# Cluster-masked attention and two feed-forward layers on one NeuronCore: how the centroids, the zero fills and the first heads' low parts are made, and a new table of priorities

## The chip, the core and the metric

The kernel runs on one core of one Trainium2 chip. The metric is the time of one execution in device microseconds, smaller is better; the kernel before takes 782.38 us (median of 3 runs, 782.28 to 784.3). A core has a TensorE for matmuls (PE in the profile, PEld for its weight loads), VectorE (DVE), ScalarE (ACT), GpSimd (POOL) and SyncE (SP), which here only issues DMA transfers. Each engine works through its own queue in order and waits for the others by semaphores.

## The reference

Attention in which a query sees only the keys of its own cluster, and then two feed-forward layers on the 1536 tokens that come out:

```
B, H, S, D, C = 2, 8, 768, 64, 16                  # 16 heads of 768 rows
q_n, k_n, c_n = normalised rows of q, k and the centroids [H, C, D]
q_assign = argmax(q_n @ c_n.T); k_assign = argmax(k_n @ c_n.T)
scores = where(q_assign == k_assign, q @ k.T / sqrt(D), -1e9)
attn = softmax(scores)                             # max subtracted, sum + 1e-9
x = (attn @ v) as [1536, 512]
h = x @ w_in                  # w_in [512, 2048]
x = (h - tanh(h)) @ w_out     # w_out [2048, 512]
out = (sigmoid(x @ w_gate) * (x @ w_val)) @ w_out2 # [512, 1536], [1536, 512]
```

All of it is in float32. The norm of a query row does not change its argmax, so the kernel normalises only the centroids.

## The kernel before

**Precision.** Most matmuls work on two parts: a high part, which is the number cast to a shorter format (fp32r or f16), and a low part, which is the number less its high part. A product is then two or three matmuls. So scores need the high parts of queries and keys (ScalarE, L737 or L748) and the low parts (GpSimd, L741 or L758); probabilities need a high part in f16 (ScalarE's second exponential of a tile) and a low part, which is the first exponential less the high part (L1022 and L1070; GpSimd or VectorE, see below); values need a high part (ScalarE, L913) and a low part (VectorE, L916), both scaled by a power of two `sv` that belongs to the pair of heads.

**Attention.** Work goes by pairs of heads (`pair_prep`, eight times) and then by heads. For a pair, queries and keys are loaded (L710), transposed by TensorE (L721), evacuated by ScalarE (L725), multiplied with the scaled centroids `cb` (L772), and VectorE makes one-hot rows of the largest of 16 scores (L781 to L792). TensorE transposes the one-hot rows (L863), and ScalarE writes them, times a large constant, into the tile `stk` (L867) below the queries and keys: a score matmul over `stk` then gives the masked score in one go. The first pair writes its high and low parts into `stk` straight from ScalarE and GpSimd (L737, L741); the later pairs go by way of `hlq`, `hlk` and DMA copies. The tile `stk_0` and its fellows are zeroed at the start, since the first pair's score matmuls run over rows that nothing writes.

Head 0 is done with queries as rows: for each of six tiles of 128 queries, six matmuls of three terms write the scores into a PSUM bank pair (L1003), VectorE takes the row maximum (L1011), ScalarE does two exponentials with it as bias (L1006), GpSimd or VectorE the low part (L1022), and a DMA transposes the probabilities. The other heads are done with keys as rows: `head_max` computes the maxima beforehand (L936 matmuls, L940 reductions) and adds them to `stk` as a row, so that the score tiles (L1056) need only exponentials (L1059) and low parts (L1070). The products with the values are L1034 for head 0 and L1082 to L1084 for the others. The score tiles and maxima share three bank pairs, `ba`, `bb` and `bc`; `bc` exists only once the first pairs are prepared.

**Centroids.** SP loads the 128x64 tile `cn` (L625); ScalarE squares it and sums its rows, takes the root, and does one exponential on a spare column so that the table of Exp is loaded early (L628 to L630); VectorE adds 1e-6, takes the reciprocal and scales `cn` (L633 to L635); TensorE transposes it (L640), and VectorE places it in `cb` (L645).

**Order.** Every step is a task with an engine, an estimated cost, the tasks that it depends on and the buffers that it takes. `Planner.run` simulates the engines with the estimates and decides which task an engine takes next: among those that could start within a short look-ahead of the earliest one (`AHEAD`, from the `AH_` numbers), the one of least priority number. The priority is read from a table by the task's number,

```
        t.n = len(self.tasks)
        t.prio = ORDER[t.n] / 1000
```

so the priorities given in the code at `add(...)` have no effect. The order that the planner finds is then written out, and each engine runs its own part of it in that order, whatever the real durations are. TensorE is also given 110 tasks of two filler matmuls each on a spare tile (`keep_busy`, L652); they keep it active in the first 50 us.

**What decides who makes a probability's low part.** `FD` and `FO` put every sixth or so of the low parts on VectorE and the rest on GpSimd (`on_v`).

**Feed-forward layers.** L1369 and L1732 are the lines with most of their matmuls; the change touches nothing there but the order.

## Time and profile before

| | |
|---|---|
| median of 3 runs | 782.38 us (782.28 to 784.3) |
| the profiled execution | 784.97 us |
| its span, from the first to the last instruction | 782.8 us |
| mean granted TensorE clock | 0.996 |
| busy in the span: PE / PEld | 770.6 / 728.4 us (98% / 93%) |
| busy in the span: DVE / ACT / POOL | 573.6 / 457.5 / 567.1 us (73% / 58% / 72%) |
| chain that ended last | PE 93%, DVE 5%, ACT 1%, issue 1% |

How to read it: the profile shows one execution, which is a little longer than the median; what lies between its time and its span is start and end. "Busy" counts the time in which at least one instruction of the engine runs. Matmuls are pipelined: the next one starts while the one before is still draining, so TensorE can be shown busy in moments in which it starts nothing; the weight loads are shown apart. The chain of work that ended last is followed back from the last instruction to whatever released it. The granted clock is 1.00 at 2.4 GHz and 0.50 at 1.2 GHz. In the rows an arrow in brackets names the idle time before an instruction and what ended it.

### The profile page before, as it was taken

The numbers are of one execution on the slowest core, as the hardware profiler recorded it, in microseconds if no ns is written. First come the engines' busy times: TensorE is split into PE (matmuls) and PEld (weight loads), VectorE is DVE, ScalarE is ACT, GpSimd is POOL, SyncE is SP. The second block draws the span as 40 slices with busy tenths as digits, with TensorE's granted clock in tenths as the row PEclk, the third lists the DMA queues.
The fourth block names the chain that finished last, engine by engine and source line by source line (L and its number), as shares of the span: only waits on it lengthen the run. The fifth ranks groups of instructions, "written<-read, shape, count | busy, mean of one in ns | idle before, by whom it ended". The sixth has DMA issues, their size and how long they took to land.

```text
span 782.8 us, 15756 instructions
## 1 busy us (share of the span) xinstructions
PE 770.6 (98%) x5905; PEld 728.4 (93%) x5905; DVE 573.6 (73%) x1110; ACT 457.5 (58%) x883; POOL 567.1 (72%) x604
## 2 busy tenths in 40 slices
PE   7999999999999999999999999999999999999998
PEld 6988899898889999999999999999998989899997
DVE  6697878887986978877576878976465786765434
ACT  4588888889887644544554455765462635253250
POOL 6249777778979795787797699699593978665261
PEclk8999999999999999999999999999999999999999
DMA  4597755665642100422131323003220332310004
GB/s 103 133 182 157 165 128 137 145 154 133 152 129 81 59 1 0 135 69 68 54 95 41 108 68 107 14 29 107 68 82 27 98 119 69 93 63 20 1 1 161
DMA packets 75571, 69.57 MB, mean 89 GB/s; under 512 B 39252, under 2 KB 60072, under 8 KB 75496
## 3 DMA queue, kind: packets, MB, share of 16 engines
q1 hardware_dynamic: 75496, 68.58, 32.6%
q8 instruction: 46, 0.75, 0.4%
q14 instruction: 29, 0.24, 0.1%
HBM read 45.12 MB, written 3.15 MB: 62 GB/s over the span
## 4 chain that ended last, share of the span: by engine, by line
PE 93%; DVE 5%; ACT 1%; issue 1%; POOL 0%; DVEq 0%; ACTq 0%; POOLq 0%
PE over_left L1369 17%; PE over_left L1732 15%; PE sm L1732 10%; PE sm L1369 10%; PE over_right L1369 8%; PE over_right L1732 6%; PE bb L1056 3%; PE bc L1056 2%; PE ba L1056 2%; PE sm L1082 2%; PE sm L1083 2%; PE sm L1084 2%; PE sm L772 2%; PE ba L936 1%; DVE finr L940 1%; PE bc L936 1%
## 5 line engine op out<-in xcount | busy, mean ns | idle before, releaser
L1070 POOL TENSOR_TENSOR pt<-pf,pt 128x768 f16<-128x768 f32 x46 | 77.3, 1694 | 19.4 <-ACT pt L1059 9.5
L1070 POOL TENSOR_TENSOR ptt<-pf,ptt 128x768 f16<-128x768 f32 x29 | 49.8, 1723 | 13.4 <-ACT pf L1059 8.2
L1732 PE MATMUL over_left<-xh,stk 128*128 128x384 f32 x186 | 54.7, 335 | 0.0
L1369 PE MATMUL over_left<-stk,w 128*128 128x384 f32 x178 | 46.4, 337 | 0.0
L1082 PE MATMUL sm<-vs,pt 128*128 128x65 f16 x318 | 43.4, 194 | 0.2 <-DVE xl L1121 0.2
L1083 PE MATMUL sm<-vs,pt 128*128 128x64 f16 x318 | 43.2, 195 | 0.0
L1084 PE MATMUL sm<-vs,pt 128*128 128x65 f16 x318 | 42.9, 192 | 0.0
L1748 ACT ACTIVATE pf<-over_left 128x384 f32<-128x384 f32 x40 | 19.6, 489 | 33.0 <-PE over_left L1732 31.7
L940 DVE TENSOR_REDUCE finr<-ba 128x1 fp32r<-128x768 f32 x35 | 33.2, 948 | 5.6 <-PE ba L936 2.7
L1400 ACT ACTIVATE stk<-pf 128x384 fp32r<-128x384 f32 x43 | 22.3, 523 | 25.0 <-POOL pf L1803 6.9
L1402 POOL TENSOR_TENSOR oht<-pf,stk 128x384 fp32r<-128x384 f32 x23 | 23.4, 1018 | 16.5 <-ACT stk L1400 16.5
L1343 POOL TENSOR_TENSOR w<-ry,w 128x256 fp32r<-128x256 f32 x26 | 20.2, 788 | 20.5 <-ACT w L1341 15.9
L1082 PEld LDWEIGHTS <-pt 128*128 128x128 f16 x318 | 29.7, 96 | 5.4 <-issue 5.0
L940 DVE TENSOR_REDUCE finr<-bc 128x1 fp32r<-128x768 f32 x32 | 30.4, 949 | 5.9 <-PE bc L936 5.7
L1732 PEld LDWEIGHTS over_left<-xh,stk 128*128 128x128 f32 x186 | 34.3, 188 | 0.3
L1732 PE MATMUL over_left<-sum,stk 128*128 128x384 f32 x127 | 33.7, 338 | 0.0
L1056 PE MATMUL bb<-stk 112*128 112x384 f32 (+2 forms) x146 | 33.6, 353 | 0.0
L1756 ACT ACTIVATE pf<-pf 128x384 f32<-128x384 f32 x33 | 17.3, 523 | 27.7 <-DVE pf L1752 27.6
L1083 PE MATMUL sm<-vs,ptt 128*128 128x64 f16 x222 | 33.1, 195 | 0.0
L1402 POOL TENSOR_TENSOR stk<-pf,hlk 128x384 fp32r<-128x384 f32 x20 | 21.1, 1056 | 16.6 <-ACT hlk L1400 16.6
L1082 PE MATMUL sm<-vs,ptt 128*128 128x65 f16 x222 | 33.0, 193 | 0.0
L1732 PE MATMUL over_left<-xl,stk 128*128 128x384 f32 x98 | 32.8, 335 | 0.0
(617 smaller groups left out, 3135.2 us busy)
## 6 DMA issues: line engine op xcount, KB each, us to landing
vs<-in_moe_w_out_dram SPq DMA_DIRECT2D x48, 256.0 KB, 2.6
vs<-in_moe_w_in_dram SPq DMA_DIRECT2D x24, 256.0 KB, 2.6
vs<-in_moe_w_val_dram SPq DMA_DIRECT2D x24, 256.0 KB, 2.7
vs<-in_moe_w_gate_dram SPq DMA_DIRECT2D x24, 256.0 KB, 2.9
stk<-hlq SPq DMA_DIRECT2D x28, 192.0 KB, 2.7
stk<-hlk SPq DMA_DIRECT2D x14, 384.0 KB, 4.4
rawq<-in_q_dram SPq DMA_DIRECT2D x16, 192.0 KB, 3.3
rawk<-in_k_dram SPq DMA_DIRECT2D x16, 192.0 KB, 3.7
```

Of the source, the lines that this page charges most:

```text
L940: rd.append(use(mx, add(DVE, c_dve(S), z + t, lambda t=t, mx=mx: nc.vector.tensor_reduce(at(mh)[:, t:t + 1], at(mx)[:, :, 0:HALF], axis=AX ...
L1056: nc.tensor.matmul(o, at(sk)[0:n, l_, ts], at(sk)[0:n, m_, c], start=i == 0, stop=i == len(terms) - 1)
L1070: lambda nce=nc.vector if on_v else nc.gpsimd, pf=pf, pt=pt: nce.tensor_tensor(at(pt)[:, 1], at(pf), at(pt)[:, 0], op=ALU.subtract), [e0, ...
L1082: nc.tensor.matmul(oview()[:, t], ph, vv[:, 0:D + 1], start=(kt == 0), stop=False)
L1083: nc.tensor.matmul(oview()[:, t, 0:D], ph, vv[:, D + 1:2 * D + 1], start=False, stop=False)
L1084: nc.tensor.matmul(oview()[:, t], plo, vv[:, 0:D + 1], start=False, stop=(kt == T - 1))
L1343: e1 = add(POOL, c_pool(PIECE), z, lambda o=o, cut=cut: nc.gpsimd.tensor_tensor(at(w[1])[:, o], f32_of(cut), at(w[0])[:, o], op=ALU.subtra ...
L1369: nc.tensor.matmul(ps, a, b, start=(i == 0), stop=(i == n - 1))
L1400: a = add(ACT, c_acts(CH), z, lambda: nc.scalar.activation(hi(), src(), AF.Copy), deps, take)
L1402: nc.vector if on_v else nc.gpsimd).tensor_tensor(lo(), src(), hi(), op=ALU.subtract), [a], port=True)
L1732: nc.tensor.matmul(at(bank[to])[:, 0:CH], lh, rh, start=start and i == 0, stop=stop and i == 3 * KH - 1, skip_group_check=True)
L1748: t = use(bank[n], add(ACT, c_act(CH), rank[0], lambda: nc.scalar.activation(at(x), ps(n), AF.Copy), [dep], [x]))
```

## The change

Six things change.

1. The centroids are loaded from ScalarE's queue, by an instruction that stands ahead of everything else there, and no longer by SP. ScalarE then does a root on a 1x1 tile `warm`, which loads the table of Sqrt.
2. Squaring and row sums of the centroids go from ScalarE (one instruction) to VectorE (a product and a reduction); ScalarE keeps the root, and then does an exponential on `warm`, which loads the table of Exp.
3. The zero fills: VectorE's three fills of 96 rows by 3072 become one of 64 rows by 1536 (on `stk_0`); GpSimd gets one of 64 rows by 3072 (on `stk_1`); `stk_2` is no longer zeroed. One of GpSimd's three fills of a row of ones (L609, 1x768) goes. Two additions to the dependencies see to it that the first two heads get these two tiles.
4. The low parts of the values of the first two pairs: ScalarE scales the raw values in place (a second instruction per head), and GpSimd subtracts the high part. Before, VectorE did both in one instruction.
5. The low parts of the probabilities of heads 0 and 1 are all made by GpSimd.
6. The table of priorities and the look-aheads are new, for the whole program.

The core of the diff; of the table, which has some 200 lines, one line of each is shown:

```diff
-    QUEUE=2.4, AH_PE=0.1147, AH_ACT=0.2895, AH_DVE=0.0311, AH_POOL=2.0837, AH_SP=1.2656, N_BUSY=110, NR=2,
+    QUEUE=2.4, AH_PE=0.1341, AH_ACT=0.2597, AH_DVE=0.0796, AH_POOL=1.2134, AH_SP=1.1231, N_BUSY=110, NR=2,
...
-    NAT=2, TB=1, ZN=2.791, ZNL=-12.734, NDV=0, EU=1, ZUD=-29.266, ZU=-22.481, ZUS=-19.807, NEW=0, ZEW=-3.275)
+    NAT=2, TB=1, ZN=2.791, ZNL=-12.734, NDV=0, LV0=2, SVP=2, ZEX=0, ZVP=0, CNA=1, ZNF=1, SQ=1, EU=1,
+    ZUD=-29.266, ZU=-22.481, ZUS=-19.807, NEW=0, ZEW=-3.275)
...
-417530 418242 418201 418201 418914 418873 418873 419250 419209 419209 419586 419545 419545
+417530 415395 418201 418201 416067 418873 418873 416403 419209 419209 416739 419545 419545
...
-    for i in range(NS):
-        if PRM["NAT"]:
-            nc.vector.memset(tiles["stk", i].bitcast(F32)[0:96].rearrange("p a n -> p (a n)"), 0.0)
+    if PRM["NAT"]:
+        nc.vector.memset(tiles["stk", 0].bitcast(F32)[D:2 * D, 2:4].rearrange("p a n -> p (a n)"), 0.0)
+        nc.gpsimd.memset(tiles["stk", 1].bitcast(F32)[0:D].rearrange("p a n -> p (a n)"), 0.0)
+    for i in (2, 0) if PRM["NAT"] else range(NS):
         nc.gpsimd.memset(tiles["stk", i].bitcast(F32)[96:97, 3, :], 1.0)
...
+    warm = const.tile([1, 1], F32, name="warm")
+    nc.vector.memset(warm, 0.0)
...
-    t_cl = add(SP, DMA_C, -199, lambda: dma(cn, centroids.rearrange("h c d -> (h c) d")), lat=0.2)
+    nc.scalar.dma_start(cn, centroids.rearrange("h c d -> (h c) d"))
+    nc.scalar.activation(warm, warm, AF.Sqrt)
 
     def cn_square():
-        nc.scalar.activation(sq, cn, AF.Square, accum_out=ss)
-        nc.scalar.activation(ss, ss, AF.Sqrt)
-        nc.scalar.activation(sq[:, 0:1], sq[:, 0:1], AF.Exp)
+        nc.vector.tensor_tensor(sq, cn, cn, op=ALU.mult)
+        nc.vector.tensor_reduce(ss, sq, axis=AX.X, op=ALU.add)
...
-    t_c1 = add(ACT, 3.0, -30, cn_square, [t_cl])
+    t_c0 = add(DVE, 0.3, -30, cn_square)
+    t_c1 = add(ACT, 0.3, -30, lambda: nc.scalar.activation(ss, ss, AF.Sqrt), [t_c0])
+    add(ACT, 1.5, PRM["ZEX"], lambda: nc.scalar.activation(warm, warm, AF.Exp), [t_c1])
     t_c2 = add(DVE, 0.5, -30, cn_scale, [t_c1])
...
-                a = add(ACT, c_acts(S), zn, lambda xt=xt, sk=sk, rw=rw, x=x: nc.scalar.activation(
-                    at(sk)[rw, x], at(xt)[rw], AF.Copy), ev[nm] + own[hh][1:2], [sk] if len(own[hh]) == 1 else [])
+                def cast(xt=xt, sk=sk, rw=rw, x=x, hh=hh):
+                    assert sk.item == hh
+                    nc.scalar.activation(at(sk)[rw, x], at(xt)[rw], AF.Copy)
+
+                a = add(ACT, c_acts(S), zn, cast, ev[nm] + own[0][1:2] + own[hh][1:2], [sk] if len(own[hh]) == 1 else [])
...
+                first_own[:] = [own[1][1]]
...
-            ts = [part(64, lambda sk=sk, hi=hi: copy(at(sk)[0:64, 0], hi("q")), hi_t["q"], hl["q"], [sk])]
+            ts = [part(64, lambda sk=sk, hi=hi: copy(at(sk)[0:64, 0], hi("q")), hi_t["q"] + first_own, hl["q"], [sk])]
...
+            if s < PRM["SVP"]:
+                a2 = add(ACT, c_acts(T * D), z + PRM["ZVS"] + PRM["ZVP"] + hh, lambda hh=hh: nc.scalar.activation(
+                    at(rv)[:, hh], at(rv)[:, hh], AF.Copy, scale=sv[:, s:s + 1]), [a])
+                c = add(POOL, c_pool(T * D), z + PRM["ZVS"] + 1 + hh, lambda hh=hh: nc.gpsimd.tensor_tensor(
+                    at(vs)[:, hh, :, D + 1:2 * D + 1], at(rv)[:, hh], at(vs)[:, hh, :, 0:D], op=ALU.subtract), [a2], port=True)
+                use(rv, a, a2, c)
+                vts.append([a, c])
+                continue
...
-                on_v = int((z + 1) * PRM["FD"] + PRM["FO"]) > int(z * PRM["FD"] + PRM["FO"])
+                on_v = h >= PRM["LV0"] and int((z + 1) * PRM["FD"] + PRM["FO"]) > int(z * PRM["FD"] + PRM["FO"])
```

The last pair of lines stands twice, for head 0 and, with `n` for `z`, for the other heads.

How the order moves is shown at three places. In all of them a row names the line (the lines after the change are 3 to 20 higher than before), the operation and what it writes and reads; `xtq_122` and `xtk_125` are the transposed queries and keys, `rawq_121` and `rawk_124` the loaded ones, `stk_86` and `stk_87` the tiles of heads 0 and 1.

**The start.** First TensorE, before: the first transposes of queries and keys with fillers among them, and the transpose of the centroids (`cn`) behind the last of them.

```order
L721 MATMUL ba_76<-ident,rawq_121 128x128 x3
...
L721 MATMUL bb_80<-ident,rawk_124 128x128 x3
...
L721 MATMUL ba_76<-ident,rawq_121 128x128 x3
L721 MATMUL bb_80<-ident,rawk_124 128x128 x3
L640 MATMUL smr_84<-ident,cn 64x128
```

TensorE at the same place after the change:

```order
L648 MATMUL smr_84<-ident,cn 64x128
...
L729 MATMUL ba_76<-ident,rawq_121 128x128 x6
...
L729 MATMUL bb_80<-ident,rawk_124 128x128 x3
...
L784 MATMUL smr_85<-cb,xtq_122 128x96 x3
L729 MATMUL bb_80<-ident,rawk_124 128x128 x3
```

The transpose of the centroids has moved from behind all four groups to ahead of all of them; before it stand 18 fillers, and ten more between it and the query transposes.

ScalarE before, from its first evacuation to the last one-hot row of the first pair:

```order
L725 ACTIVATE xtq_122<-ba_76 128x384
L725 ACTIVATE xtk_125<-bb_80 128x384
L737 ACTIVATE stk_86<-xtq_122 64x768
L737 ACTIVATE stk_86<-xtk_125 64x768
L737 ACTIVATE stk_87<-xtq_122 64x768
L737 ACTIVATE stk_87<-xtk_125 64x768
L913 ACTIVATE vs_89<-rawv_92,sv 128x6x64 x2
L867 ACTIVATE stk_87<-smr_85 16x768
L867 ACTIVATE stk_86<-smr_84 16x768
...
L867 ACTIVATE stk_86<-sm_71 16x768
L867 ACTIVATE stk_87<-smr_84 16x768
```

ScalarE after:

```order
L733 ACTIVATE xtk_125<-bb_80 128x384
L747 ACTIVATE stk_86<-xtk_125 64x768
L747 ACTIVATE stk_87<-xtk_125 64x768
L925 ACTIVATE vs_89<-rawv_92,sv 128x6x64
L929 ACTIVATE rawv_92<-rawv_92,sv 128x384
L925 ACTIVATE vs_89<-rawv_92,sv 128x6x64
L879 ACTIVATE stk_87<-sm_71 16x768
L879 ACTIVATE stk_86<-smr_85 16x768
L879 ACTIVATE stk_86<-smr_84 16x768
L879 ACTIVATE stk_87<-sm_71 16x768
```

One scaling of the values has come between the two value casts, and the four one-hot rows now follow each other, those of head 0 (`stk_86`) second and third.

**Head 0's score tiles.** TensorE before, from head 0's third score tile on (L1003, by banks), with the maxima of the next heads (L936) between:

```order
L1003 MATMUL ba_76<-stk_86 128x384 x6
L936 MATMUL bc_632<-stk_87 128x384 x2
L721 MATMUL sm_72<-ident,rawk_124 128x128 x3
L721 MATMUL sm_71<-ident,rawk_124 128x128 x3
L1003 MATMUL bb_80<-stk_86 128x384 x6
L949 MATMUL bc_632<-ident,finr_114 1x128 x6
L936 MATMUL ba_76<-stk_88 128x384 x2
L721 MATMUL sm_72<-ident,rawq_121 128x128 x3
L1003 MATMUL bc_632<-stk_86 128x384 x6
```

TensorE after, from head 0's third tile on (L1023); the second, further up, is also in `bb`:

```order
L1023 MATMUL bb_80<-stk_86 128x384 x6
L956 MATMUL ba_76<-stk_87 128x384 x2
...
L1023 MATMUL bb_80<-stk_86 128x384 x6
L729 MATMUL sm_71<-ident,rawk_124 128x128 x3
L956 MATMUL ba_76<-stk_88 128x384 x2
L969 MATMUL bc_622<-ident,finr_114 1x128 x6
...
L1023 MATMUL ba_76<-stk_86 128x384 x6
L729 MATMUL sm_71<-ident,rawq_121 128x128 x3
L956 MATMUL bc_622<-stk_88 128x384 x2
L1023 MATMUL bb_80<-stk_86 128x384 x6
```

Head 0's six tiles went through the banks `ba`, `bb`, `ba`, `bb`, `bc`, `bb`; now they go through `ba`, `bb`, `bb`, `bb`, `ba`, `bb`, and the maxima use `ba` in between.

**GpSimd.** Its queue before, from the low parts of the second pair's queries to head 1's first probability tiles (L1070):

```order
L758 TENSOR_TENSOR hlq_123<-xtq_122,hlq_123 128x384 x2
L1022 TENSOR_TENSOR pt_96<-pf_107,pt_96 128x768
L758 TENSOR_TENSOR hlk_126<-xtk_125,hlk_126 128x384 x2
L1022 TENSOR_TENSOR pt_100<-pf_109,pt_100 128x768
L1022 TENSOR_TENSOR pt_102<-pf_107,pt_102 128x768
L1022 TENSOR_TENSOR ptt_104<-pf_108,ptt_104 128x768
L1022 TENSOR_TENSOR ptt_105<-pf_109,ptt_105 128x768
L1070 TENSOR_TENSOR ptt_106<-pf_107,ptt_106 128x768
```

The same stretch after (L931 are the values' low parts):

```order
L931 TENSOR_TENSOR vs_89<-rawv_92,vs_89 128x6x64
L770 TENSOR_TENSOR hlq_123<-xtq_122,hlq_123 128x384 x2
L770 TENSOR_TENSOR hlk_126<-xtk_125,hlk_126 128x384
L931 TENSOR_TENSOR vs_89<-rawv_92,vs_89 128x6x64
L770 TENSOR_TENSOR hlk_126<-xtk_125,hlk_126 128x384
L1042 TENSOR_TENSOR pt_96<-pf_107,pt_96 128x768
L1042 TENSOR_TENSOR pt_98<-pf_108,pt_98 128x768
L1042 TENSOR_TENSOR pt_100<-pf_109,pt_100 128x768
L931 TENSOR_TENSOR vs_90<-rawv_92,vs_90 128x6x64 x2
L1042 TENSOR_TENSOR pt_102<-pf_107,pt_102 128x768
L1042 TENSOR_TENSOR ptt_104<-pf_108,ptt_104 128x768
L1042 TENSOR_TENSOR ptt_105<-pf_109,ptt_105 128x768
```

Four subtractions for the values and one more low part of head 0 (`pt_98`) have come in ahead of head 1's tiles.

## Rows read from the trace of the kernel before

**Rows 1.** The page's head and its part 1: busy us, share, instructions.
```profile
span 782.8 us, 15756 instructions
...
PE 770.6 (98%) x5905; PEld 728.4 (93%) x5905; DVE 573.6 (73%) x1110; ACT 457.5 (58%) x883; POOL 567.1 (72%) x604
```

**Rows 2.** Stretches: us long, busy us of each engine (x instructions), granted clock, DMA.
```profile
10.00:20.00 10.00, 7.01 (x48) 6.95 (x48) 5.83 (x15) 3.30 (x5) 7.94 (x5) 0.66 0.36 80
60.00:250.00 190.00, 187.72 (x2422) 170.14 (x2421) 155.62 (x277) 165.92 (x251) 156.82 (x109) 1.00 0.58 139
350.00:400.00 50.00, 50.00 (x289) 50.00 (x288) 33.46 (x74) 22.97 (x53) 37.90 (x48) 1.00 0.19 60
```

**Rows 3.** Timeline to 26 us: start, us (of a group: in all), engine, line.
```profile
0.75 1.38 SPq L710 DMA_DIRECT2D rawq<-in_q_dram  x2
...
2.16 2.62 DVE L608 MEMSET stk<- 96x3072 f32 x1 [0.20 <-issue]
...
2.17 0.64 SPq L625 DMA_DIRECT2D cn<-in_centroids_dram  x1
...
2.76 2.08 POOL L609 MEMSET stk<- 1x768 f32 x3
...
4.95 0.77 PE L721 MATMUL ba<-ident,rawq 128*128 128x128 f32 x3 [0.57 <-POOL stk L609]
5.00 0.26 ACT L628 ACTIVATE sq<-cn 128x64 f32<-128x64 f32 x1 [2.98 <-DMA cn<-in_centroids_dram]
...
5.37 1.28 ACT L629 ACT_TABLE_LOAD   x1
...
6.67 0.20 ACT L629 ACTIVATE ss<-ss 128x1 f32<-128x1 f32 x1
...
8.29 0.47 ACT L725 ACTIVATE xtq<-ba 128x384 f32<-128x384 f32 x1
8.57 2.62 DVE L608 MEMSET stk<- 96x3072 f32 x1 [0.59 <-issue]
...
10.17 0.83 ACT L737 ACTIVATE stk<-xtq 64x768 fp32r<-64x768 f32 x1
...
11.08 3.68 POOL L741 TENSOR_TENSOR stk<-xtq,stk 64x768 fp32r<-64x768 f32 x2 [5.91 <-ACT stk L737]
...
11.45 1.49 DVE L635 TENSOR_SCALAR cn<-cn,ss 128x64 f32<-128x64 f32 x1
...
13.20 1.49 PE L652 MATMUL sm<-busy 128*128 128x128 bf16 x12
...
20.73 1.12 ACT L913 ACTIVATE vs<-rawv,sv 128x384 f16<-128x384 f32 x2 [7.40 <-DVE sv L682]
...
22.64 1.62 ACT L867 ACTIVATE stk<-smr 16x768 fp32r<-16x768 bf16 x2 [0.79 <-PE smr L863]
...
26.18 1.32 PE L1003 MATMUL ba<-stk 80*128 80x384 f32 x6
```

**Rows 4.** Timeline from 26 us on, the first scores of head 0.
```profile
27.53 0.96 DVE L1011 TENSOR_REDUCE fin<-ba 128x1 f32<-128x768 f32 x1 [4.46 <-PE ba L1003]
...
27.98 1.96 POOL L758 TENSOR_TENSOR hlq<-xtq,hlq 128x384 fp32r<-128x384 f32 x2 [8.68 <-ACT hlq L748]
...
28.68 0.91 ACT L1006 ACTIVATE pt<-ba,fin 128x768 f16<-128x768 f32 x1
...
30.75 0.60 PE L936 MATMUL bb<-stk 128*128 128x384 f32 x2
...
31.07 0.56 DVE L781 TENSOR_REDUCE mm<-smr 128x24 f32<-128x384 f32 x1 [1.73 <-PE smr L772]
...
50.90 1.21 PE L1056 MATMUL ba<-stk 128*128 128x384 f32 x6
```

**Rows 5.** Page part 5, GpSimd's costliest group; timeline of TensorE at 67 us.
```profile
L1070 POOL TENSOR_TENSOR pt<-pf,pt 128x768 f16<-128x768 f32 x46 | 77.3, 1694 | 19.4 <-ACT pt L1059 9.5
...
67.99 0.20 PE L1082 MATMUL sm<-vs,ptt 128*128 128x65 f16 x1
```

More of the change, by code (lines that the diff above doesn't have):

```diff
@@ L689, in tile_cluster_attention_moe @@
     K2 = 97
-    stk, mready, mrow, vready = {}, {}, {}, {}
+    stk, mready, mrow, vready, first_own = {}, {}, {}, {}, []
     ramp = [t_cb]
@@ L1067, in head_attend @@
                 n = T * h + t
-                on_v = int((n + 1) * PRM["FD"] + PRM["FO"]) > int(n * PRM["FD"] + PRM["FO"])
+                on_v = h >= PRM["LV0"] and int((n + 1) * PRM["FD"] + PRM["FO"]) > int(n * PRM["FD"] + PRM["FO"])
                 x = add(DVE if on_v else POOL, c_dve(S) if on_v else c_pool16(S), z + PRM["ZLOW" if on_v else "ZLOWP"],
```

406 rows, old and new, of the table ORDER are left out of this document.

## The prediction

> **What bounds the kernel now.** I read the page's head first, then stretches, the start in order of time, and who waits there. TensorE is busy for 98% of the span [rows 1], so time can only come from TensorE waiting less or running at the higher clock. The stretches tell where that is possible. Matmuls overlap, so the busy share hides short waits and I go by the weight loads (PEld). At 350 to 400 us they fill the whole stretch: nothing to gain. At 60 to 250 us they fill 170.14 of 190 us: some 20 us of small waits. In 10 to 20 us TensorE is busy for 7.01 of 10 us and its granted clock averages 0.66, so much of it ran at 1.2 instead of 2.4 GHz [rows 2].
>
> The first score tile, L1003, starts at 26.18 us; until then TensorE does fillers (L652), transposes and centroid scores [rows 3]. The rows of the start, read backwards, name the chain. L1003 needs the one-hot rows that ScalarE writes (L867, from 22.64). These need the cluster scores (L772), which need the centroids, scaled only at 11.45 + 1.49 = 12.94. The centroid load left SP at 2.17 and its data was used at 5.00, the root needed a table load of 1.28, and then VectorE was in its third zero fill until 8.57 + 2.62 = 11.19. The scaling itself took 1.49 because GpSimd's first subtraction (11.08, 1.84 each) held it: it ended right with that. ScalarE then waited 7.40 us for `sv`, before 20.73 [rows 3].
>
> **The change part by part.** Call c the time at which the scaled centroids are ready; it is 12.94 now.
>
> *How early c becomes.* ScalarE issues the load at 0.75, as SP issues its first one; with the same 2.83 us (2.17 to 5.00) it lands at 3.6. VectorE's first fill started at 2.16 and its third at 8.57, 3.2 for each; the one that stays is half as long, 1.6, then comes the 1x1 fill: free at about 4.1 [rows 3]. The square and the sum over 64 elements are not in the trace; a reduction of 384 takes 0.56 [rows 4], so I take 0.15 each. With the root (0.2 [rows 3]), three hand-overs of 0.2 and 0.5 for the three scaling steps, c = 5.6. The other end: GpSimd now zeroes 64x3072. Its three fills of 768 take 2.08 [rows 3], so by free size the new one takes 2.8, from 2.76 to 5.6. If it holds VectorE's square for all that time, that is 1.3 more, and if the last scaling step is held as now (1.49 for 0.15) 1.3 more: c = 8.2. I take 6.4, nearer to the lower end since fills are not subtractions. The Sqrt table now loads before the data is there, and Exp's while the transposes run; both cost nothing, unless c falls under 4.
>
> The row shows VectorE held by a GpSimd subtraction. The Trainium skill ("GPSIMD Engine Reference", Key points) says that GpSimd shares its SBUF interfaces with VectorE, and that the contention is with instructions of two SBUF inputs or in a two-port mode. The 1.49 us agrees; by that rule the new square, with two SBUF inputs beside GpSimd's fills, lies at the late end. That is a rival below.
>
> *A wait is added.* In TensorE's order the centroid transpose now stands ahead of the first query transposes. Behind it wait ten fillers (12 take 1.49 at the lower clock) and two groups of three transposes (0.77 each) [rows 3]: with the transpose itself the queries are out at c + 2.7. Queued behind are the key transposes, and ScalarE waits for them.
>
> *From there to the first score tile.* ScalarE from c + 2.9: four evacuations of 0.48 and four casts of 0.83 [rows 3], 5.3 in all, to c + 8.2. Then two value casts of 0.56 and the new scaling of the values in place, 1.7, to c + 9.9; `sv` is ready at about c + 7.3 by the order, so the 7.40 us wait goes. Then four one-hot rows of 0.8 (two in 1.62): head 0 has its own after the third, c + 12.3. The key one-hots come 0.6 us before ScalarE wants them, so ScalarE is what is late next. With three query transposes, the first tile starts at c + 12.7 = 19.1 instead of 26.18: 7.1 earlier [rows 3].
>
> *From the first tile to head 1's first exponent tile* (L1056, now at 50.90). The order puts tiles 2, 3 and 4 of head 0 all into bank bb, and head 1's maxima into ba. Rows: a reduction 0.96, an exponential 0.91, a max matmul pair 0.60, a one-hot step 0.56 [rows 4]; a cast 0.83 and six score matmuls 1.1 (1.32 with the last one's drain) [rows 3]. After c + 13.1 ScalarE does four evacuations, a cast and tile 1's two exponentials, 4.6: c + 17.7. Bank ba gets the next max pair, which is out at c + 18.6; from there VectorE has four reductions and three one-hot steps, 4 x 0.96 + 3 x 0.56 = 5.5, the last being tile 2's: c + 24.1. Tiles 3 and 4 in the same bank each need exponentials 1.8, hand-overs 0.5, matmuls 1.1, a reduction 1.0, and tile 3 also six transposes before it: together 9.0, c + 33.1. Tile 5 waits for one more reduction, then 1.2 + 1.1: c + 36.4; its exponentials, behind a row copy, evacuations and tile 4's second one, end at c + 38.7, and L1056's bank is free at c + 38.9 = 45.3. That is 5.6 earlier than 50.90. But the order then has six score matmuls and three transposes fewer behind it (1.1) and four fillers still ahead (0.2): 4.3 us gained for TensorE. Ends for c of 5.6 and 8.2: 5.1 and 2.5.
>
> *What is hidden.* VectorE loses four low parts of the values and two of the probabilities; GpSimd gets them. ScalarE gets four value scalings. All lie before 68 us beside the chain above, except the one counted.
>
> *The new order.* The table is new to the end of the program, and TensorE's matmuls are the same in number: 5905. Its worth lies in 60 to 250 us. If these became as dense as 350 to 400, 20 us would go; nothing in the rows excludes a loss of like size. I take 1.7 gained, under a tenth.
>
> *Sum.* The profiled execution took 784.97 (span 782.8 and 2.2 around it): 784.97 - 4.3 - 1.7 = 779.0. The median of the runs, 782.38, is 0.9967 of that execution, so 776.4.
>
> The skill ("Perfetto Trace Analysis", Identifying the Most-Contended Engine) also says to judge TensorE's room by weight loads and not by matmul time. By the loads the room in 60 to 250 us is 20 us, by matmul time 2.3; were the latter right, the 1.7 would fall to 0.2 and the sum would be 777.9.
>
> **The rivals.** *Slower: GpSimd becomes the bound.* Place: from head 0's low parts to the first value matmul of head 1 (L1082 on ptt, 67.99). It gets four value subtractions, for which I take its rows of like size, 0.98 [rows 4], and two low parts of 1.69 [rows 5], 7.3 us. For it: four of these stand ahead of head 1's low parts in its queue, and TensorE's order is fixed behind L1082. Against it: GpSimd stood idle 19.4 us before its low parts [rows 5]. It decides when GpSimd has no gap left there. Then 7.3 - 4.3 = 3.0 are lost: 784.97 + 3.0, scaled, 785.3.
>
> *The port.* The fills hold the square and the scaling fully, c = 8.2, and the order gives nothing: 784.97 - 2.5, scaled 779.9.
>
> *All is kept.* The 7.1 us at the first tile stay, since banks turn faster than my serial count, and the order gives 5: 784.97 - 12.1, scaled 770.3. For it: VectorE has less to do from 26 to 51. Against: tiles 2 to 4 share a bank.
>
> *Given back.* The start gains 4.3, but 60 to 250 us becomes a little less dense, 166 instead of 170 of 190: no change, 782. For it: an order that is searched for estimated costs can be late anywhere.
>
> **How the numbers follow.** Chances: forecast 0.45, all kept 0.15, port 0.15, given back 0.10, slower 0.15. The forecast's own range is 773 to 780. The range from 768 to 785.5 leaves out about 0.07 below and 0.10 above. A measurement can tell 0.3%, 2.35 us, from no change. Faster (below 780.0): forecast, all kept, and most of the port's case, 0.71. Same: given back and the rest of the port, 0.13. Slower: 0.16.
>
> **What would show it.** Right: scaled centroids at 5.6 to 8.2; ScalarE without a long wait before the value casts; L1003's successor at 18.5 to 21 and L1056's at 44 to 48. The loads in 60 to 250 us, between 168 and 174 of 190, show what the order is worth. Wrong: a centroid transpose after 9, which holds the queries; a first score tile after 23; or GpSimd without gaps up to 68 us and TensorE waiting there for a low part.

## The result and the profile after

The changed kernel is slower: 791.76 us (median of 12 runs, 784.86 to 795.75) against 784.14 us for the kernel before, run beside it, ratio 1.0080 (95% interval 1.0052 to 1.0107). A second series gave 787.68 (11 runs, 785.34 to 793.04), ratio 1.0058 (1.0035 to 1.0081). The forecast was 776.4, in a range from 768.0 to 785.5. The changed kernel also spreads over 8 to 11 us, where the runs of before lie mostly between 781.2 and 786.

The first trace of the changed kernel shows its shortest execution, 784.86 us. The page's head and part 1:

```profile
span 783.1 us, 15773 instructions
...
PE 769.6 (98%) x5905; PEld 726.4 (93%) x5905; DVE 563.8 (72%) x1105; ACT 460.2 (59%) x885; POOL 575.1 (73%) x610
```

The same stretches as in [rows 2], of this trace:

```profile
10.00:20.00 10.00, 9.54 (x109) 8.71 (x110) 4.29 (x16) 9.62 (x16) 8.82 (x6) 1.00 0.33 74
60.00:250.00 190.00, 184.43 (x2442) 167.63 (x2440) 158.05 (x279) 161.34 (x247) 152.76 (x108) 1.00 0.58 138
350.00:400.00 50.00, 50.00 (x288) 50.00 (x287) 34.43 (x76) 24.49 (x57) 38.13 (x46) 1.00 0.18 59
```

At 10 to 20 us TensorE is at the full clock and busier. At 60 to 250 us its loads fill 167.63 of 190 us where [rows 2] had 170.14: the new order is thinner there, not denser.

The timeline of the start, as in [rows 3], and head 1's first tile, as in [rows 4]:

```profile
0.75 0.37 ACTq L631 DMA_DIRECT2D cn<-in_centroids_dram  x1
...
2.32 1.34 DVE L610 MEMSET stk<- 64x1536 f32 x1 [0.36 <-issue]
...
2.65 2.65 POOL L611 MEMSET stk<- 64x3072 f32 x1
...
3.70 0.22 DVE L635 TENSOR_TENSOR sq<-cn 128x64 f32<-128x64 f32 x1
...
4.83 0.53 DVE L641 TENSOR_SCALAR cn<-cn,ss 128x64 f32<-128x64 f32 x1
...
5.50 0.39 PE L648 MATMUL smr<-ident,cn 128*64 128x128 f32 x1 [2.41 <-DVE cn L641]
...
13.54 0.62 ACT L925 ACTIVATE vs<-rawv,sv 128x384 f16<-128x384 f32 x1
...
18.48 1.29 PE L1023 MATMUL ba<-stk 80*128 80x384 f32 x6
...
43.31 1.30 PE L1076 MATMUL ba<-stk 128*128 128x384 f32 x6
```

The centroids are scaled at 5.36, the first score tile starts at 18.48 (26.18 before) and head 1's first tile at 43.31 (50.90 before). So the start does what the prediction said, and a little more. The time goes later.

**How far ahead is it?** I use one measure throughout, the lead. Each matmul that is no filler counts with the usual time from its start to the next start for its shape (the lower quartile over the traces); the table says how much earlier than in the second trace of before (experiment c1) a kernel had started the same sum of work. Minus is later.

| at (us of c1) | before, first trace | changed, first trace | changed, second trace (a1) | old start, new order (b3) | new start, old order from 21 us (b2) | new order to 45 us, then old (d1) | changed, five subtractions moved (e1) |
|---|---|---|---|---|---|---|---|
| 26.2 | -3.7 | +3.9 | +3.9 | -2.5 | +0.5 | +3.9 | +3.9 |
| 40 | -3.7 | +2.4 | +2.4 | -4.0 | 0.0 | +2.4 | +2.4 |
| 50 | -3.7 | +0.7 | +0.6 | -6.1 | 0.0 | +0.2 | +0.7 |
| 100 | -3.6 | -0.8 | -1.3 | -6.1 | +0.1 | +0.3 | -1.2 |
| 180 | -3.7 | -1.2 | -3.1 | -6.3 | -0.8 | +0.3 | -1.2 |
| 260 | -3.6 | -2.3 | -5.9 | -8.4 | -0.7 | +0.2 | -2.4 |
| 350 | -3.7 | -3.0 | -7.4 | -10.3 | -1.1 | -0.1 | -3.1 |
| end | -3.6 | -3.9 | -8.4 | -11.5 | -1.4 | -0.1 | -4.0 |

Three things are in it. The trace on which the forecast rested was of a long execution, 3.7 us behind another of the same kernel from the start on. Of the lead at the first score tile almost nothing is left at 50 us, whatever the order. And behind 50 us the old order loses 0.3 to 1.4 us (d1 and b2), the new one 4 to 9.

### The profile page after: what moved, and what is told of

Read it like the earlier page. It is cut to its first block, busy times and chain, and to the rows that moved or that the text cites. A ratio compares the mean times of both kernels' runs of the same rounds, so it can differ in the third digit from the quotient of the medians.

```text
span 783.1 us, 15773 instructions
## 1 busy us (share of the span) xinstructions
PE 769.6 (98%) x5905; PEld 726.4 (93%) x5905; DVE 563.8 (72%) x1105; ACT 460.2 (59%) x885; POOL 575.1 (73%) x610
## 4 chain that ended last, share of the span: by engine, by line
PE 89%; DVE 6%; ACT 3%; issue 1%; DMA 1%; POOL 0%; DVEq 0%; ACTq 0%; SPq 0%; POOLq 0%
PE over_left L1389 18%; PE over_left L1752 14%; PE over_right L1389 11%; PE over_right L1752 11%; PE sm L1752 5%; PE sm L1389 5%; PE ba L1076 3%; PE bb L1076 2%; PE bc L1076 2%; PE sm L1102 2%; PE sm L1103 2%; PE sm L1104 2%; PE sm L784 2%; PE sm L660 1%; PE bc L956 1%; DVE finr L960 1%
## 5 line engine op out<-in xcount | busy, mean ns | idle before, releaser
L1752 PE MATMUL over_left<-xh,stk 128*128 128x384 f32 x148 | 45.6, 336 | 0.1
L1772 DVE TENSOR_TENSOR pf<-over_left,pf 128x384 f32<-128x384 f32 x42 | 23.3, 554 | 24.7 <-PE over_left L1752 12.3
L960 DVE TENSOR_REDUCE finr<-bb 128x1 fp32r<-128x768 f32 x32 | 30.4, 949 | 9.1 <-PE bb L956 7.6
L1389 PE MATMUL over_left<-stk,w 128*128 128x384 f32 x140 | 36.7, 337 | 0.0
L1102 PE MATMUL sm<-vs,ptt 128*128 128x65 f16 x228 | 33.1, 193 | 0.1
L1102 PEld LDWEIGHTS <-pt 128*128 128x128 f16 x312 | 29.2, 96 | 4.0 <-issue 3.8
L1104 PE MATMUL sm<-vs,ptt 128*128 128x65 f16 x228 | 32.8, 191 | 0.0
L1076 PE MATMUL ba<-stk 112*128 112x384 f32 (+2 forms) x128 | 29.6, 354 | 1.7 <-DVE finr L960 1.2
L1389 PE MATMUL over_left<-w,stk 128*128 128x512 f32 x104 | 30.6, 394 | 0.0
L1752 PE MATMUL over_right<-xh,stk 128*128 128x384 f32 x96 | 30.0, 336 | 0.0
L1104 PEld LDWEIGHTS <-pt 128*128 128x128 f16 x312 | 29.7, 99 | 0.0
L1103 PEld LDWEIGHTS <-pt 128*128 128x128 f16 x312 | 29.4, 97 | 0.1
L1076 PE MATMUL bc<-stk 112*128 112x384 f32 (+2 forms) x128 | 29.4, 352 | 0.0
```

The source lines that it names most:

```text
L960: rd.append(use(mx, add(DVE, c_dve(S), z + t, lambda t=t, mx=mx: nc.vector.tensor_reduce(at(mh)[:, t:t + 1], at(mx)[:, :, 0:HALF], axis=AX ...
L1076: nc.tensor.matmul(o, at(sk)[0:n, l_, ts], at(sk)[0:n, m_, c], start=i == 0, stop=i == len(terms) - 1)
L1102: nc.tensor.matmul(oview()[:, t], ph, vv[:, 0:D + 1], start=(kt == 0), stop=False)
L1103: nc.tensor.matmul(oview()[:, t, 0:D], ph, vv[:, D + 1:2 * D + 1], start=False, stop=False)
L1104: nc.tensor.matmul(oview()[:, t], plo, vv[:, 0:D + 1], start=False, stop=(kt == T - 1))
L1389: nc.tensor.matmul(ps, a, b, start=(i == 0), stop=(i == n - 1))
```

## The experiments

In the kernels of b1 to b4, c2 to c4, d1 to d3 and e1, e2 the planner's search is replaced by a list of its steps and of the buffers that they take, and each engine follows its part of the list; the rest is the changed kernel, but for the edit shown. Ratios are to runs of the kernel before that were made beside the kernel in question.

**a1. The changed kernel again.** No edit.

> The changed kernel as it is, for a trace of one of its longer executions: of its twelve runs five took 784.9 to 788.8 us and seven 791.6 to 795.8, and only one of the first kind (784.86, granted clock 1.00 throughout) was seen in a trace. Theory A (a transfer is late): the longer executions wait longer for a load of keys or for the copies into stk between 55 and 90 us, where the trace of the short one has TensorE waiting for rawk (62.49) and the DMA engines busy for 0.79 to 0.97 of the time; a longer execution then shows 4 to 8 us more of start-to-start gaps there, and its lower clock behind the gap. Theory B (the clock): the work before 50 us, with its gap of 2.72 us at 2.78, lets the granted clock fall to about half in one or two places before 50 us, and real matmuls run slower there; a longer execution then shows no longer waits, but a stretch with a granted clock well under 1 where real matmuls run.

787.68 us. The trace is of an execution of 789.33. Up to 65 us it is the first one again; then it is late at single places: 172, 244 and 322 us, besides the 206 us of both. Its clock is 1.00 throughout, so theory B fails for this execution; theory A's places (55 to 90) fail too. It is none of the longest: in the first series the five runs up to 788.8 us have a mean granted clock of 1.00, the seven from 791.6 us on 0.993 to 0.998, and of those seven no trace exists. TensorE's waits from 40 to 335 us (line waited for, releaser: us in total, times, longest), in this trace:

```profile
PE sm L1102 <- DVE pf L1464: 1.5, 1, 1.5
PE over_left L1752 <- DVE pf L1772: 1.4, 1, 1.4
PE ba L1076 <- DVE finr L960: 1.3, 1, 1.3
PE sm L835 <- DVE oh L804: 1.2, 1, 1.2
```

All four end with VectorE, but not for one reason. Ahead of the second, at 322 us, VectorE had itself waited for weights, which were ready 4.54 us after their load was issued; in the first trace it did not have to wait there, 3.34 us after the issue. So 1.4 us of this execution is a late transfer, though not where theory A had it:

```profile
320.72 0.43 DVE L1334 TENSOR_SCALAR over_left<-vs 128x256 uint32<-128x256 uint32 x1 [1.15 <-DMA vs<-in_moe_w_in_dram]
```

Ahead of the other three, one of VectorE's subtractions took much longer than usual. What VectorE did ahead of the last of them (`oh`, at 172 us), in the first trace, where TensorE did not wait there:

```profile
169.25 1.63 DVE L936 SCALAR_TENSOR_TENSOR vs<-rawv,sv,vs 128x384 f16<-128x384 f32 x1
```

in a1, with the wait that followed, and GpSimd at the time:

```profile
169.74 3.24 DVE L936 SCALAR_TENSOR_TENSOR vs<-rawv,sv,vs 128x384 f16<-128x384 f32 x1
...
169.30 3.27 POOL L1090 TENSOR_TENSOR pt<-pf,pt 128x768 f16<-128x768 f32 x2
...
173.30 0.52 PE L835 MATMUL sm<-ident,oh 128*64 128x128 bf16 x6 [1.21 <-DVE oh L804]
```

and in the trace of b4 (below), whose lines are numbered 14 higher:

```profile
170.07 6.43 DVE L950 SCALAR_TENSOR_TENSOR vs<-rawv,sv,vs 128x384 f16<-128x384 f32 x1
...
169.63 3.25 POOL L1104 TENSOR_TENSOR pt<-pf,pt 128x768 f16<-128x768 f32 x2
172.86 3.22 POOL L1104 TENSOR_TENSOR ptt<-pf,ptt 128x768 f16<-128x768 f32 x2
...
176.82 0.85 PE L849 MATMUL sm<-ident,oh 128*64 128x128 bf16 x6 [4.41 <-DVE oh L818]
```

It is the same subtraction, which takes 0.61 us where GpSimd rests. GpSimd has four subtractions of 1.6 to 2.0 us back to back there. VectorE's one ends about 0.4 us after GpSimd's first, second or fourth ends; which of them, differs from one execution to the next. I call such an instruction held.

**b1 to b4. The parts by themselves.** The edits:

```diff
 b1: order = first 115 steps of the changed kernel (to its first score tile), then the order of before
-    LV0=2, SVP=2, CNA=1, ZNF=1
+    LV0=0, SVP=0, CNA=1, ZNF=1
 b2: the order as b1; LV0=2, SVP=2, CNA=1, ZNF=1
 b3: the order of the changed kernel; centroids and zero fills as before
+    LV0=2, SVP=2, CNA=0, ZNF=0
 b4: the order of the changed kernel; low parts as before
+    LV0=0, SVP=0, CNA=1, ZNF=1
```

> The changed kernel's start (centroids from ScalarE's queue, squares on VectorE, the new fills, its order up to about the first score tile of head 0), and from there on the order of before, word for word on each engine; the low parts of values and probabilities made where they were before. What is told apart: in the trace of the changed kernel TensorE is 7.6 us ahead of before (at equal matmul work) at 26 to 40 us, 4.4 at 60, 2.7 at 90 to 200, 1.2 at 220 and nothing at the end; in a second trace it fell another 4.4 us back, at VectorE instructions at 172, 244 and 322 us. Theory 1 (the new order after the start loses it): here 4 to 7 us of the lead stay to the end, 776 to 779 us. Theory 2 (an earlier start runs into transfers and buffers that can't come earlier, whatever the order): the lead is gone by 100 us, 781 to 784. Theory 3 (the low parts on GpSimd): as theory 1, 776 to 779.

> As the run before, the changed kernel's start and then the order of before, but with the low parts of the first two pairs' values and of heads 0 and 1's probabilities on GpSimd, as in the change, at the places in its queue where the order of before has them. Theory 1 (the new order loses the lead): 776 to 780. Theory 2 (transfers): 781 to 784. Theory 3 (GpSimd's added 7 us are on the path): 3 us or more above the run without them, 780 to 786, and TensorE behind from 30 to 70 us.

> The order of the changed kernel on every engine, and its low parts on GpSimd, but the centroids loaded by SP, squared on ScalarE, and the three zero fills on VectorE as before, so that the scaled centroids come at about 13 us again. Theory 1 (the new order loses some 8 us against the old one after the start, whenever it starts): the late start comes on top, 790 to 797. Theory 2 (the lead would be lost to transfers anyway): little later than the changed kernel, 785 to 790. Theory 3 (GpSimd): as theory 1.

> The changed kernel with its order on every engine, but the low parts of the first two pairs' values on VectorE (without ScalarE's second scaling) and those of heads 0 and 1's probabilities divided between VectorE and GpSimd as before. Theory 1 (the order): as the changed kernel, 785 to 793. Theory 2 (transfers): the same. Theory 3 (GpSimd's added work): 778 to 782.

b1 782.77 us (10 runs, 782.14 to 783.23; ratio to before 0.9992, 0.9974 to 1.0010), b2 781.55 (10 runs, 0.9984, 0.9963 to 1.0004), b3 795.96 (4 runs, 1.0152, 1.0106 to 1.0198), b4 793.19 (4 runs, 1.0111, 1.0062 to 1.0160). b2 and the changed kernel differ in the order behind 21 us alone, and by 6 to 10 us (6 to 7.5 by the ratios): the order loses it, as theory 1 says, and b3 and b4, which have the new order, are as slow as theory 1 has them (b4 0.2 us above its range). But b1 and b2 do not end at 776 to 780: of the new start nothing is left against before, as theory 2 says for the first 50 us; that transfers are the reason is not shown. Theory 3 fails on both sides: with the low parts on GpSimd it is not slower, rather 1 us faster (b2 and b1).

**c1. Before again.** No edit.

> The kernel before, unchanged, for a second trace of it. The first trace is of an execution of 784.97 us, in which the clock fell to 1.2 GHz between 10 and 20 us; other executions of it took 781 to 782.5 us. If the fall is what the longer ones pay for, a shorter one has the granted clock at 1.00 (or a shorter fall), and is 2 to 3 us ahead of the first trace at equal matmul work from 26 us on, and then stays so; the gain that the change has at the start is then only some 5 us against it, not 7.6. If the longer ones lose their time elsewhere, the two agree up to 26 us.

781.32 us. Its start, for the rows that differ from [rows 2, 3]:

```profile
0.00:10.00 10.00, 7.09 (x66) 6.73 (x67) 7.38 (x5) 5.36 (x9) 4.28 (x34) 0.87 0.48 121
10.00:20.00 10.00, 9.13 (x111) 8.29 (x110) 8.18 (x24) 6.15 (x10) 7.37 (x4) 0.96 0.36 80
...
11.45 0.25 DVE L635 TENSOR_SCALAR cn<-cn,ss 128x64 f32<-128x64 f32 x1
...
22.50 1.30 PE L1003 MATMUL ba<-stk 80*128 80x384 f32 x6
```

The scaling that took 1.49 us took 0.25 here, the clock at 10 to 20 us was granted at 0.96 instead of 0.66 (with a shorter fall, 0.87, ahead of it), and the first score tile started at 22.50 instead of 26.18. The expectation holds: the difference of 3.65 us between the two executions of before lies ahead of 26 us and stays. One run; but of the 23 runs of before beside d1, eight took 781.2 to 782.4, fourteen 783.6 to 785.2 and one 788.1: two groups about as far apart as the two traces.

**c2, c3. VectorE's held instructions moved back.** The edits:

```diff
 c2: the changed kernel's order, on VectorE only:
-    vlow(6,1), hot(6,1), max(63), end(8), max(65), max(64)
+    hot(6,1), max(63), end(8), max(65), max(64), vlow(6,1)
 c3: as c2, and three low parts of probabilities likewise, two to four places back
```

> The changed kernel with one VectorE instruction moved: the low part of the seventh pair's second head's values (at 169 us) goes five places back in VectorE's queue, behind the one-hot rows, a normalisation and three row maxima that stood behind it. In three traces of the same order it took 1.63, 3.24 and 6.43 us, ending each time when one of GpSimd's back-to-back instructions ended, and TensorE then waited for the one-hot rows behind it (gaps of up to 4.6 us). Theory (order): VectorE instructions that need the port shared with GpSimd are caught at random in the new order, and what stands behind them on VectorE is urgent: the gap at 172 us goes, the median falls by 1 to 3 us, to 785 to 789, and the spread gets smaller, but the waits at 206, 244 and 322 stay. Rival (transfers late at random): median and spread as before the move, 787 to 793.

> The changed kernel with four VectorE instructions moved two to five places back in VectorE's queue, nothing else: the one of the run before, and the low parts of probabilities at 65.7, 204.3 and 240.6 us, which took 2.5, 2.4 and 0.95 to 2.4 us instead of 0.95 while GpSimd worked. Behind them stood row maxima, the row for the next head, and the high part for which TensorE waited at 206 and 244 us. Theory (order): the waits of TensorE at 69, 172, 206 and 244 us shrink by 0.5, 1.5 to 4.5, 1.5 and 0 to 1.5 us; 781 to 786. Rival (transfers): as the changed kernel, 785 to 793.

795.14 and 795.16 us (6 runs each): no gain, rather a loss. In both traces the gap at 172 us is gone, but a new one of 3.2 us stands at 179 to 188. TensorE's longest waits in c2:

```profile
PE sm L700 <- DVE vm L696: 2.9, 1, 2.9
PE sm L989 <- DVE finr L974: 2.7, 1, 2.7
```

The first is my edit: the moved subtraction is the last reader of `rawv`, which has one buffer. The next pair's values are loaded later, VectorE sat idle 3.7 us for that load (3.6 in c3), and TensorE waited for the maximum `vm`. So neither run separates the theory from its rival. The second is a place that I had not moved; VectorE's low part there was held for 4.57 us under three of GpSimd's:

```profile
94.45 4.57 DVE L1104 TENSOR_TENSOR ptt<-pf,ptt 128x768 f16<-128x768 f32 x1
...
93.34 4.86 POOL L1104 TENSOR_TENSOR pt<-pf,pt 128x768 f16<-128x768 f32 x3
...
98.94 0.94 DVE L974 TENSOR_REDUCE finr<-ba 128x1 fp32r<-128x768 f32 x1
```

Behind such a wait the clock falls too; the stretches of c2 before and after it (the granted clock is the third number from the end):

```profile
90.00:100.00 10.00, 7.33 (x101) 6.37 (x99) 9.00 (x13) 6.89 (x10) 8.20 (x6) 0.97 0.49 98
100.00:110.00 10.00, 9.97 (x104) 9.52 (x105) 4.35 (x6) 5.32 (x9) 3.30 (x3) 0.69 0.59 129
```

A gap of 3.04 us cost 5.7 us of lead, from +2.8 to -3.0 against the first trace of before. In c3 no low part took over 1.9 us, and it was no faster: besides the load, TensorE waited there for 1.9 us at 215 us for an exponential of ScalarE. Holds are not all that the new order loses by.

**c4. Fewer fillers behind the first tile.** The edit, on b2:

```diff
-    N_BUSY=110
+    N_BUSY=81      # 42 tasks behind the first tile (40 in the kernel before)
```

> As the run with the changed kernel's start, the order of before behind it and the low parts on GpSimd, but with 58 of the 220 filler matmuls left out, so that behind the first score tile as many remain as in the kernel before, at the places that they had there. In that run TensorE was 7.5 us ahead of before at 26 us and 4.2 at 30, where fillers that had not been done before the first tile stood in one piece. Theory (the fillers took it): the lead at 30 us is 6 to 7.5 us, and 778 to 780 us at the end. Rival (what follows the first tile is held by VectorE and ScalarE, not by fillers): the lead is gone by 35 us all the same, 781 to 783; or the clock falls for want of them, 782 to 785.

781.86 us (12 runs, 780.86 to 784.25). At 30 us the lead was there (7.5 us on the first trace of before); then TensorE waited 2.2 us in one piece, the granted clock was 0.80 and 0.86 in the next two stretches of 10 us, and at 36 us the lead was 2.1. Its four runs with a mean granted clock of 1.00 took 780.9 to 782.1 us, so it is not the fall of the clock alone that keeps it there. Fillers were not what took the lead; without them the waits show.

**d1 to d3. Where the new order loses.** The edit is the list alone:

```diff
 d1: first 280 steps of the changed kernel, then the order of before
 d2: first 351 steps, then the order of before
 d3: as d1 as far as the planner's 150 us, then the changed kernel's order again
```

> The changed kernel with its own start, low parts and order for the first 280 steps of the planner (on TensorE up to about 33 us, head 0's first four score tiles), and from there the order of before. At that point the trace of the changed kernel is 4.2 us ahead of the second trace of before (7.9 of the first). Theory 1 (the new order loses the lead after 40 us, the old one keeps what it is given, as it kept 3 us in the two runs with the old order behind the start): 3 to 4 us of the lead stay, 778 to 780. Theory 2 (transfers that can't come earlier): the lead over the second trace of before is gone by 60 us, 781 to 784.

> As the run before, with the changed kernel's order for its first 351 steps (up to about 45 us). Its trace lost 2.7 us of lead between 40 and 45 us, where head 0's last tiles and head 1's first ones go through the banks. Theory 1: what is lost there stays lost and nothing after it, 779 to 782, 1 to 3 us above the run before. Theory 2: as the run before, 781 to 784.

> As the run with the new order up to 40 us, but only as far as the steps that the old order has before about 160 us; from there the changed kernel's order again. Theory 1, by places: the new order loses 1.5 us at 206 us in every trace and another 1.4 to 4.6 at 172, 1.5 at 244 and 1.5 at 322 in some, so this lies between the run before and the changed kernel, 781 to 788, with the changed kernel's spread. Theory 2: 782 to 785 with little spread.

In the traces TensorE keeps the changed kernel's order up to 44.6 us in d1 and up to 57.2 us in d2, later than the expectations say.

d1 781.16 us (12 runs, 781.00 to 781.82; ratio 0.9969, 0.9953 to 0.9986), d2 781.78 (0.9977, 0.9961 to 0.9992), d3 791.34 (6 runs, 1.0088, 1.0057 to 1.0119). d1 beats both kernels, and hardly varies: with the clock at 1.00 in its first 30 us it always ends where before ends in its short executions. It does not beat those, and its lead of some 3.5 us at 35 us is down to 1.6 at 45, still in the new order, and to 0.2 at 50: so far theory 2, though what takes the lead was not found. d2 lies in both its ranges and decides nothing. d3 has the old order's calm up to 156 us (lead +0.3) and loses behind it, to -6.1 at 180 and -12.1 at 700; but its 791.34 us lie above both ranges. Some 4 us of that come from one place that no trace of the changed kernel has, where the two orders are joined: at 156 us TensorE waited 2.4 us for an exponential of ScalarE, and the granted clock was 0.84 over the next 10 us. From 180 us on d3 loses 6 us, as a1 does (5): theory 1 for what follows. The waits of TensorE between 40 and 335 us in d1, its four longest:

```profile
PE sm L700 <- ACT xtk L747: 0.6, 1, 0.6
PE sm L1150 <- DVE xl L1155: 0.4, 1, 0.4
PE sm L700 <- DVE mt L991: 0.3, 1, 0.3
PE bb L970 <- ACT ptt L1093: 0.3, 1, 0.3
```

**e1. Five subtractions off VectorE.** The edit, on the changed kernel with its order:

```diff
-                on_v = h >= PRM["LV0"] and int((n + 1) ...
+                on_v = h >= PRM["LV0"] and T * (h - 1) + t not in (7, 19, 68, 87) and int((n + 1) ...
-            if s < PRM["SVP"]:
+            if s < PRM["SVP"] or (s, hh) == (6, 1):
```

> The changed kernel with five of VectorE's subtractions given to GpSimd, at the same steps of the order: the low parts of probabilities seen held on VectorE in one trace or another (at 65.7, 94.4, 204.3 and 240.6 us) and that of the seventh pair's second head's values (169 us; with ScalarE's scaling in place, as the change does it for the first two pairs). Theory 1a (in the new order VectorE's two-input subtractions are caught between back-to-back GpSimd instructions, and urgent work stands behind them): the gaps of TensorE at 69, 172, 206 and 244 us shrink, the median is 781 to 786 and the spread under 4 us. Rival 1b (the new order is too tight in other ways too, so that any late instruction, also GpSimd's 8 us more of work, makes TensorE wait): 786 to 793, with gaps at other places.

785.55 us (12 runs, 783.80 to 790.25; ratio 1.0040, 1.0021 to 1.0059), 2 to 6 us under the changed kernel by the medians, eleven of the runs at 787.2 or less, the spread 6.5 us and not under 4. Against the first series of the changed kernel that is clear; against the second (1.0035 to 1.0081) the intervals overlap. Its trace has no loss at 172 and 244 us (table), as the first trace of the changed kernel has none; what stays, in the longest waits of its trace, is of the kind that both traces of the changed kernel share:

```profile
PE bc L1090 <- DVE finr L974: 1.2, 1, 1.2
PE bb L970 <- ACT pf L1093: 1.0, 1, 1.0
PE sm L743 <- DMA rawk<-in_k_dram: 0.8, 1, 0.8
```

So theory 1a has most of the varying part, and 1b the constant 4 us: row maxima, exponentials and one load of keys that come too late in the new order. The row maxima at least are late behind a hold again. At 206 us in the changed kernel, and at 217 us in e1, where a low part that had not been moved was caught, VectorE worked without a pause from the held instruction to the maximum for which TensorE waits:

```profile
204.27 2.42 DVE L1090 TENSOR_TENSOR ptt<-pf,ptt 128x768 f16<-128x768 f32 x1
...
212.85 2.40 DVE L1104 TENSOR_TENSOR pt<-pf,pt 128x768 f16<-128x768 f32 x1
```

The first row is of the first trace of the changed kernel, the second of e1; free, such an instruction takes 0.95 us. Why the exponentials and the keys are late was not taken apart.

**e2. d1 with fewer fillers.** The edit: `N_BUSY=94`, the 16 tasks taken from behind the first tile.

> The steadiest kernel so far (the changed kernel's order for its first 280 steps and the order of before behind it) with 32 of its 220 filler matmuls left out, every other pair of those behind the first score tile. There the first tile is 4.2 us earlier than in the shorter execution of before, yet at 50 us only 0.3 us of matmul work is ahead; 62 more fillers are left over at the first tile. If these fillers take TensorE's time (32 x 0.055 = 1.8 us), the result is 779 to 780. If they only fill time in which TensorE would wait for VectorE and ScalarE, it is 781 to 782, with waits where the fillers were; if the clock falls for want of them, 782 to 786.

781.29 us (12 runs, 781.05 to 782.58): as d1. In the traces fillers between 20 and 50 us went from 8.0 to 6.2 us and TensorE's waits from 3.4 to 5.2 us: they only fill waits.

## Why the prediction was wrong

- **The early centroids: right.** c was 5.36, even under the early end of 5.6. GpSimd's fill did not hold the square (0.22), and the scaling only for the rest of the fill (0.53; it ended 0.06 behind it). The port's rival, 8.2, fails.
- **From c to the tiles: right.** The first tile came at c + 13.1 (predicted c + 12.7), head 1's first at c + 38.0 (c + 38.9). ScalarE's wait for `sv` went. Against the first trace of before the lead at 45 us is 5.2 us (1.5 + 3.7, by the measure of the table), a little more than the 4.3 of the sum.
- **First failed step: "The median of the runs, 782.38, is 0.9967 of that execution, so 776.4."** The 2.6 us by which the profiled execution was longer were not spread over it. They lay in the very start that the change replaces: a fall of the clock from 12 to 19 us and a held scaling, where the short execution that was traced has half that fall and no hold (c1). Against a short execution the start is worth 3.9 us at the first tile and 0.2 to 0.7 at 50 us. The row of the clock at 0.66 [rows 2] was read as what the start costs; it was what that one execution cost. And a lead at a tile is not a lead in work: at the first tile only 78 of the 220 fillers were done (140 in c1), and TensorE's waits of the first 20 us (start to start, beyond the usual time of each shape) were 6.7 against 7.0 us. The tile came earlier for fillers put off rather than for waits saved, and without these fillers TensorE only waits (e2).
- **Second failed step, and the larger: "I take 1.7 gained, under a tenth."** The new order lost 4.6 us between 50 us and the end in its best execution (+0.7 to -3.9) and 9.0 in the next; b2, the same without it, lost 1.4. The prediction had said that nothing in the rows excluded a loss; it took a gain all the same, and gave the loss ("given back") a chance of 0.10 and 4 us, where it was 6 to 10. The sum closes with it: 784.97 - 4.3, and then 4.6 or 9.0 lost, gives 785.3 and 789.7, and the two traced executions took 784.86 and 789.33. The mechanism under it, an order searched for estimated costs that is late anywhere, is what the runs show. The port was priced for the start only [rows 3], though the same row, 1.49 us for a step of 0.25, showed that it could cost something anywhere.
- **Where the new order loses.** One place is VectorE: two-input subtractions that are held behind GpSimd's, ahead of work that TensorE needs. That they are held is not new. In the first trace of before, 9 of VectorE's 32 low parts took over 0.5 us more than when free, the longest 1.79 us instead of 0.95, and TensorE had no gap of over 0.7 us between 40 and 335 us; in the first trace of the changed kernel it was 9 of 26, the longest 2.52, and in other traces with its order 3.24, 4.57 and 6.43 (a1, c2, b4). New are the length and what stands behind. The rest of the loss, for ScalarE's exponentials and for loads, was seen (c3, d3, a1) and not explained.
- **GpSimd as the bound: did not come.** Its added low parts cost nothing (b1, b2). Where it decided, it was as the one that held VectorE up, and not as the one that TensorE waited for.
- The signs named for a wrong forecast (transpose after 9, first tile after 23, GpSimd without gaps) all concerned the start. Only the loads at 60 to 250 us, 167.63 where 168 to 174 were to be right, pointed to it.

## What to carry to other kernels

Look at the spread of the runs before scaling a profiled execution to their median, and ask in which stretch the profiled one was long: a second trace, which costs one run, can tell. A new order of a whole program is judged by what stands behind instructions whose duration can vary, not by how full the engines are; one held instruction on an engine that is a quarter idle cost as much (5.7 us in c2) as the whole gain aimed at (4.3 + 1.7). A tile that starts earlier is worth only the waits that it saves: here 3.9 us at the first tile were 0.2 to 0.7 at 50 us.

## What had not been expected of the hardware

- VectorE's subtraction of two SBUF inputs (0.61 us free) took 1.63, 3.24 and 6.43 us in three executions under GpSimd's back-to-back subtractions. The Trainium skill ("GPSIMD Engine Reference", Key points) says that the two engines share SBUF interfaces and contend in such instructions; these traces agree, and show besides that the wait is for an end of one of GpSimd's instructions, not always the first, so that one place in the program has several durations.
- A wait of TensorE of 3 us cost nearly twice its length, with a lower granted clock behind it (0.69 over 10 us in c2). Waits of 1.2 to 1.5 us, as in a1, cost about their length, at a clock of 1.00.
- GpSimd's zero fill of 2.65 us let VectorE's product of two inputs through (0.22 us), but the scaling behind it took 0.53 instead of 0.25 us and ended with the fill (5.36 and 5.30).
